# Batch 0 of an attention backward: rows of q and grad_out moved to SP's queue, and V's pieces transposed in another order

## The chip, the core and the metric

The kernel runs on one core of one Trainium2 chip. A core has TensorE (PE, with its weight loads shown apart as PEld), VectorE (DVE), ScalarE (ACT), GpSimd (POOL) and SyncE (SP), each with its own stream of instructions, and 16 DMA engines that all of them share. The metric is the device time of one execution in microseconds. Where a profile is shown, it is of one execution, and it gives the clock that TensorE was granted, as a share of its full speed.

## The reference

Attention with grouped heads, forward and backward, in bfloat16: 32 batches, 32 query heads, 4 key and value heads, 4 query positions, 2048 keys, head size 128. Eight query heads share a key head, so a batch has 128 query rows, 32 for each key head.

```python
def _fwd_reference(q, k, v):
    ...
    k = jnp.repeat(k, rep, axis=1)
    v = jnp.repeat(v, rep, axis=1)
    scale = D ** -0.5
    scores = jnp.einsum("bhqd,bhkd->bhqk", q, k) * scale
    p = _softmax(scores, axis=-1)
    return jnp.einsum("bhqk,bhkd->bhqd", p, v)

def reference(q, k, v, grad_out):
    ...
    _out, _vjp = jax.vjp(_f, q, k, v)
    _grads = _vjp(grad_out)
```

The outputs are the attention's output and the gradients of q, k and v. K and V are 2 MB a batch each, and so are their gradients; q, grad_out, the output and dq are 32 KB a batch each.

## The kernel before

The kernel goes through the batches one after the other, with the stages of neighbouring batches interleaved. A batch has these steps, and the names are those of the order that is written out in the kernel:

- `LK`, `LV`: load K and V, one transfer of 512 KB for each of the four key heads, on SP's queue. K has three buffers, V two.
- `KT0` to `KT7`, `VT0` to `VT7`: transpose K and V, in eight pieces each. A piece is eight 128x128 transposes on PE into one bank of PSUM, and one copy of 128x1024 to SBUF, by DVE, or by ACT where the name ends in `a`. Pieces with an even number are of heads 0 and 1, odd ones of heads 2 and 3.
- `QDT`: transpose q and grad_out. `Sa`, `Sb`: the two halves of the scores, and their row maxima on DVE (`m`); the second one also makes the bias of the exponentials (`negb`).
- `EXa`, `EXb`: the exponentials on ACT, with their row sums. `ETa`, `ETb`: their transposes on PE, and copies on DVE.
- `NRM`: the sum and the inverse of the row sums on DVE (`rinv`), then on POOL grad_out times `rinv` (`dop`, four instructions of 32 rows) and q times the scaled inverse (`qp`).
- `dV0` to `dV7`: the gradient of V from E and `dop`. `O`: the output, from E's transposes and V, and `delta`. `dPa`, `dPb`: grad_out times the transposed V, and the gradient of the scores (`ds`). `dSTa`, `dSTb`, `dQ`, `dK0` to `dK7`: the rest.

Every engine carries out its instructions in the order in which the text lists the steps; there is no scheduler behind it. `HEAD` (lines 17 to 25) lists the steps up to the third batch, `STEADY` one iteration of the middle, `TAIL` the end. A step is `name@batch`. PSUM has eight banks; a step takes one or two and gives them back once they are copied out, so a transpose may wait for a copy.

What matters for the first batch:

- q and grad_out come in groups of four batches (`GROUP`, line 192). The first group is loaded from ACT's queue in four transfers: 32 KB of q and of grad_out for batch 0, then 96 KB each for batches 1 to 3, in runs of 256 bytes. Later groups come by POOL's queue.
- Transfers from SP and ACT take turns in eight semaphores. A transfer whose semaphore is still held by an earlier one is issued only when that one has landed. In the kernel before, the four transfers of V of batch 0 wait in this way for q of batch 0, the first head of K, grad_out of batch 0, and the rows of q for batches 1 to 3; the second head of K of batch 1 waits for the rows of grad_out for batches 1 to 3.
- Ahead of the first data, PE runs 23 matmuls on the identity (line 212).

Of the kernel before, what the change touches and what calls it, by code (L numbers as in the profile page):

```python
# [14 lines left out]


HEAD = """
LK@0 LV@0 KT4@0 KT6@0 KT2@0 KT0@0 QDT@0 KT3@0 KT1@0 KT5a@0 KT7@0 LK@1 LV@1 Sa@0 Sb@0 VT2a@0 VT5@0 VT3@0 EXb@0 VT4@0 EXa@0 VT0a@0 ETb@0 ETa@0
NRM@0 VT7a@0 VT6@0 VT1a@0 QDT@1 KT4@1 KT6@1 KT2a@1 KT0@1 KT3@1 dV7@0 O@0 dV5@0 dPb@0 dV1@0 KT5@1 KT1@1 dV3@0 dV6@0 dPa@0 KT7@1 dV2@0 LK@2 LV@2
VT2@1 dV4@0 Sa@1 dV0@0 Sb@1 dK7@0 VT5@1 VT3@1 EXb@1 dSTa@0 VT4@1 EXa@1 VT0@1 QDT@2 dSTb@0 KT4@2 dK1@0 dK6@0 KT6@2 KT2@2 KT0@2 NRM@1 dK0@0 dQ@0  # L20
dK3@0 dK5@0 dK2@0 ETb@1 ETa@1 VT7@1 KT3@2 VT6@1 VT1@1 dV7@1 dK4@0 O@1 dV5@1 dPb@1 dV1@1 KT5@2 KT1@2 dV3@1 dV6@1 dPa@1 KT7@2 dV2@1 LK@3 LV@3
VT2@2 dV4@1 Sa@2 dV0@1 Sb@2 dK7@1 VT5@2 VT3@2 EXb@2 dSTa@1 VT4@2 EXa@2 VT0@2 QDT@3 dSTb@1 KT4@3 dK1@1 dK6@1 KT6@3 KT2@3 KT0@3 NRM@2 dK0@1 dQ@1
# [84 lines left out]
def kernel(ctx: ExitStack, tc: tile.TileContext, q, k, v, grad_out, out_0, out_1, out_2, out_3):  # L107
    nc = tc.nc
# [8 lines left out]
    W = 4  # L117
# [32 lines left out]
    q_f = q.rearrange("b h s d -> b (h s) d")  # L150
    go_f = grad_out.rearrange("b h s d -> b (h s) d")
# [10 lines left out]
    def late():  # L162

        return "v" in st.get(B - 1, {})
# [6 lines left out]
    def counted(n, i, *transfers):  # L171
        if late():
            return
        ends[n, i] = True
        for t in transfers:
            t.then_inc(sems[n][i % 4], 16)
            tc.no_tile_sem_insts.add(t.ins.name)
            tc.add_to_no_dep_group(f"{n}.{i}", t.ins)
            counts[n][i % 4] += 16
# [10 lines left out]
    groups = {}  # L190

    def GROUP(g, queue):

        groups[g] = []
        for name in ("q_sb", "do_sb"):
            groups[g].append(qd_pool.tile([P, W, D], BF16, name=name))
        for a, b in ((0, 1), (1, W)) if g == 0 else ((0, W),):
            for x, src in zip(groups[g], (q_f, go_f)):
                t = queue.dma_start(out=x[:, a:b], in_=src[g * W + a:g * W + b].rearrange("w p d -> p w d"))
                if g:  # L200
                    counted("qdo", g, t)

    def LK(b):
        S = st[b] = {}
        if b == 0:
            GROUP(0, nc.scalar)

            first = sm_pool.tile([P, 1], FP32, name="first")
            nc.scalar.activation(out=first[:], in_=ident[:, 0:1], func=ACT.Exp)
            t = banks.take(1)  # L210
            for _ in range(WARM_MATMULS):
                nc.tensor.matmul(
                    banks.ap(t)[:, 0, 0:2 * D], lhsT=ident[:], rhs=pairs["dop", 0][:].rearrange("p a d -> p (a d)"), start=True, stop=True,
                )
            banks.give(t)
        S["q"], S["do"] = (x[:, b % W, :] for x in groups[b // W])
        if b and b % W == 0:
            fence("qdo", b // W)
        if b % W == W - 1 and b + 1 < B:
            GROUP(b // W + 1, nc.gpsimd)  # L220
        S["k"] = k_pool.tile([P, NH, C, D], BF16, name="k_sb")
        for h in range(NH):
            nc.sync.dma_start(out=S["k"][:, h].rearrange("p c d -> p (c d)"), in_=k_v[b, h])

    def LV(b):
        S = st[b]
        S["v"] = v_pool.tile([P, NH, C, D], BF16, name="v_sb")
        for h in range(NH):
            nc.sync.dma_start(out=S["v"][:, h].rearrange("p c d -> p (c d)"), in_=v_v[b, h])

    def bank16():

        t = banks.take(1)
        return t, banks.ap(t).rearrange("p a w -> p (a w)").bitcast(BF16).rearrange("p (u r) -> p u r", r=P)
# [189 lines left out]
    def dP(b, i):  # L424
# [6 lines left out]
        banks.give(t)  # L431

    table = {"LK": LK, "LV": LV, "QDT": QDT, "O": O, "dQ": dQ, "NRM": NRM}
    for i, c in enumerate("ab"):
        for n, f in (("S", S_), ("EX", EX), ("dP", dP), ("ET", ET), ("dST", dST)):
# [10 lines left out]
    for w in STEADY.split():  # L446
        ahead = 0
        for mark, n in (("+3", 3), ("+2", 2), ("+", 1), ("-2", -2), ("-", -1)):
            if w.endswith(mark):
                w, ahead = w[:-len(mark)], n  # L450
# [3 lines left out]
    with tc.manual_schedule():  # L454

        for w in HEAD.split():
            w, b = w.split("@")
# [5 lines left out]
        for w in TAIL.split():  # L463
            w, b = w.split("@")
# [33 lines left out]
```

## Time and profile before

| | |
|---|---|
| three runs, us | 682.58, 682.12, 685.99 |
| median, us | 682.58 |
| the profiled execution, us | 685.76 |
| its span from the first to the last instruction, us | 684.0 |
| mean granted TensorE clock in it | 0.994 |

The times in the profile count from the start of the span. A group of instructions is named by its line, its engine, its operation, what it writes and what it reads, with the shape and the count. A row of the chain has a start, a length and what the chain was in then. A wait is put down to the event that came last. "DMA share" is the time that packets took, as a share of 16 engines; it can pass 1 a little. For a transfer the time to landing counts from its issue.

### The profile page before, as it was taken

The numbers are of one execution on the slowest core, as the hardware profiler recorded it, in microseconds if no ns is written. First come the engines' busy times: TensorE is split into PE (matmuls) and PEld (weight loads), VectorE is DVE, ScalarE is ACT, GpSimd is POOL, SyncE is SP. The second block draws the span as 40 slices with busy tenths as digits, with TensorE's granted clock in tenths as the row PEclk, the third lists the DMA queues.
The fourth block names the chain that finished last, engine by engine and source line by source line (L and its number), as shares of the span: only waits on it lengthen the run. The fifth ranks groups of instructions, "written<-read, shape, count | busy, mean of one in ns | idle before, by whom it ended". The sixth has DMA issues, their size and how long they took to land.

```text
span 684.0 us, 28075 instructions
## 1 busy us (share of the span) xinstructions
PE 626.7 (92%) x12375; PEld 454.9 (67%) x12375; DVE 590.0 (86%) x997; ACT 569.5 (83%) x673; POOL 273.0 (40%) x457
## 2 busy tenths in 40 slices
PE   7999998999989999999999999999998999989984
PEld 5777765677666677666677666677666677666652
DVE  4899998889888888998889898889898889888895
ACT  3799897888878888988888888888888888986885
POOL 1354343543426343264443426354244542434310
PEclk9999999999999999999999999999999999999999
DMA  9999999999999999999999999999999999999888
GB/s 344 404 321 405 418 415 411 414 389 413 415 414 409 392 415 414 414 416 410 417 416 415 416 415 416 414 417 413 414 415 414 412 411 415 416 417 395 340 335 298
DMA packets 76971, 274.45 MB, mean 401 GB/s; under 512 B 8976, under 2 KB 9134, under 8 KB 76849
## 3 DMA queue, kind: packets, MB, share of 16 engines
q1 hardware_dynamic: 41120, 144.85, 53.0%
q0 software_dynamic: 34640, 127.55, 46.4%
q8 instruction: 96, 1.57, 0.8%
q10 hardware_dynamic: 1088, 0.26, 0.2%
q14 instruction: 27, 0.21, 0.1%
HBM read 136.31 MB, written 136.31 MB: 399 GB/s over the span
## 4 chain that ended last, share of the span: by engine, by line
PE 79%; DVE 6%; issue 5%; ACT 5%; DMA 3%; POOL 0%; ACTq 0%; SPq 0%; DVEq 0%; POOLq 0%
PE banks L250 32%; PE banks L386 19%; PE banks L267 9%; PE banks L333 9%; PE banks L317 8%; ACT dv L390 3%; DMA v_sb<-in_v_dram 2%; DVE ds L428 2%; ACT dk L390 2%; DVE vt L252 1%; DMA q_sb<-in_q_dram 1%; DVE kt L252 1%; PE banks L240 1%; DVE dk L390 1%; DVE m L280 1%
## 5 line engine op out<-in xcount | busy, mean ns | idle before, releaser
L390 ACT CAST dv<-banks 128x1024 bf16<-128x1024 f32 x254 | 244.3, 1027 | 60.3 <-PE banks L386 60.1
L390 ACT CAST dk<-banks 128x1024 bf16<-128x1024 f32 x251 | 246.4, 1023 | 19.1 <-PE banks L386 15.2
L252 DVE COPY kt<-banks 128x1024 bf16<-128x1024 bf16 x254 | 162.9, 679 | 14.3 <-PE banks L250 13.8
L252 DVE COPY vt<-banks 128x1024 bf16<-128x1024 bf16 x252 | 164.0, 680 | 4.6 <-PE banks L250 4.2
L250 PE MATMUL banks<-ident,v_sb 128*128 128x128 bf16 x2048 | 144.0, 220 | 16.0 <-ACT dv L390 10.1
L300 POOL TENSOR_SCALAR dop<-do_sb,rinv 32x128 bf16<-32x128 bf16 x124 | 74.1, 598 | 205.3 <-PE banks L386 152.2
L250 PE MATMUL banks<-ident,k_sb 128*128 128x128 bf16 x2048 | 143.1, 219 | 10.8 <-issue 7.3
L250 PEld LDWEIGHTS <-k_sb 128*128 128x128 bf16 x2048 | 119.4, 98 | 38.5 <-issue 37.7
L250 PEld LDWEIGHTS <-v_sb 128*128 128x128 bf16 x2048 | 122.2, 98 | 32.0 <-issue 26.0
L386 PE MATMUL banks<-dop,e 64*128 64x256 bf16 x1024 | 96.8, 274 | 8.0 <-issue 3.0
L428 DVE SCALAR_TENSOR_TENSOR ds<-banks,delta,e 128x1024 bf16<-128x1024 f32 x64 | 82.0, 1283 | 25.3 <-PE banks L267 25.3
L188 POOL DMA_DIRECT2D out_dram<-dv x56 | 39.2, 703 | 145.3 <-ACT dv L390 135.0
L386 PE MATMUL banks<-qp,ds 64*128 64x256 bf16 x1024 | 87.8, 272 | 2.9 <-DVE dk L390 1.2
L300 POOL TENSOR_SCALAR qp<-q_sb,srinv 32x128 bf16<-32x128 bf16 x128 | 77.7, 607 | 10.6
L291 ACT ACTIVATE e<-banks,negb 128x1024 bf16<-128x1024 f32 x64 | 70.7, 1111 | 11.2 <-DVE negb L283 11.1
L280 DVE TENSOR_REDUCE m<-banks 128x1 f32<-128x1024 f32 x64 | 75.2, 1213 | 1.6 <-PE banks L267 1.5
L386 PEld LDWEIGHTS <-e 64*128 64x128 bf16 x1024 | 34.0, 94 | 54.1 <-issue 37.3
L386 PEld LDWEIGHTS <-ds 64*128 64x128 bf16 x1024 | 42.1, 94 | 31.1 <-ACT dv L390 12.6
L319 DVE COPY et<-banks 128x1024 bf16<-128x1024 bf16 x64 | 41.8, 686 | 23.7 <-PE banks L317 23.3
L267 PE MATMUL banks<-vt,qdt 128*32 128x512 bf16 x512 | 41.3, 384 | 6.8 <-issue 4.3
L319 DVE COPY dst<-banks 128x1024 bf16<-128x1024 bf16 x64 | 43.4, 679 | 0.0
L267 PEld LDWEIGHTS <-qdt 128*32 128x32 bf16 x1024 | 18.9, 94 | 36.1 <-issue 34.7
(45 smaller groups left out, 505.3 us busy)
## 6 DMA issues: line engine op xcount, KB each, us to landing
k_sb<-in_k_dram SPq DMA_DIRECT2D x128, 512.0 KB, 10.9
v_sb<-in_v_dram SPq DMA_DIRECT2D x128, 512.0 KB, 16.0
out_dram<-dk POOLq DMA_DIRECT2D x29, 2048.0 KB, 19.8
out_dram<-dv POOLq DMA_DIRECT2D x17, 2048.0 KB, 20.7
out_dram<-dv POOLq DMA_DIRECT2D x13, 1024.0 KB, 18.1
out_dram<-dv POOLq DMA_DIRECT2D x13, 960.0 KB, 22.3
out_dram<-dk SPq DMA_DIRECT2D x2, 2048.0 KB, 7.6
out_dram<-dv SPq DMA_DIRECT2D x1, 2048.0 KB, 8.7
```

The costliest lines, as they stand in the source:

```text
L250: nc.tensor.transpose(out=ps[:, 4 * hh + j, :], in_=S[which][:, 2 * (i % 2) + hh, 4 * (i // 2) + j, :], identity=ident[:])
L252: copy(out=S[f"{which}t{i}"][:], in_=ps)
L267: nc.tensor.matmul(ps[G * h:G * h + G, a, :], lhsT=S["qdt"][:, col, G * h:G * h + G], rhs=xt[:, 4 * (h % 2):4 * (h % 2) + 4, :].rearrange( ...
L280: nc.vector.reduce_max(out=S["m"][:, i:i + 1], in_=S[f"s{i}"][1], axis=AX.X)
L291: nc.scalar.activation(out=S[f"e{i}"][:], in_=ps, func=ACT.Exp, bias=S["negb"][:], scale=scale, accum_out=S["l"][:, i:i + 1],)
L300: engine.tensor_scalar(out=t[r, h % 2, :], in0=src[r, :], scalar1=by[r, :], scalar2=None, op0=ALU.mult)
L317: nc.tensor.transpose(out=ps[:, u, :], in_=S[f"{src}{i}"][:, P * u:P * u + P], identity=ident[:])
L319: nc.vector.tensor_copy(out=S[f"{name}{i}"][:], in_=ps)
L333: nc.tensor.matmul(ps[G * h:G * h + G, :], lhsT=S[f"{xt}{c // 8}"][:, c % 8, G * h:G * h + G], rhs=S[kv][:, h, c, :], start=(c == 0), stop ...
L386: nc.tensor.matmul(ps[:, a, :, c, :], lhsT=S[f"{x}{i // 4}"][r, u:u + P], rhs=S[y][r, :, :], start=True, stop=True, tile_position=(2 * G * ...
L390: copy(out=S[name][:, :, 2 * i:2 * i + 2, :].rearrange("p h c d -> p h (c d)"), in_=banks.ap(t).rearrange("p a (j w) -> p (a j) w", j=2),)
L428: nc.vector.scalar_tensor_tensor(out=S[f"ds{i}"][:], in0=ps, scalar=S["delta"][:], in1=S[f"e{i}"][:], op0=ALU.subtract, op1=ALU.mult,)
```

## The change

Two things change, both for batch 0 only. The 96 KB each of q and grad_out for batches 1 to 3 are no longer issued from ACT's queue at the very start but from SP's, behind the four transfers of the first V and ahead of K of batch 1. The turns in the eight semaphores shift with that: of the first V's four transfers the first two now take fresh semaphores, and the other two wait for q of batch 0 and for the first head of K. And in `HEAD` the V pieces of heads 0 and 1 (4, 0 and 6, behind 2 as before) come first, with the exponentials between them; the pieces of heads 2 and 3 follow, 5 and 3 of them between the transposes of E, and piece 6 is no longer behind `NRM`.

```diff
 HEAD = """
-LK@0 LV@0 ... LK@1 LV@1 Sa@0 Sb@0 VT2a@0 VT5@0 VT3@0 EXb@0 VT4@0 EXa@0 VT0a@0 ETb@0 ETa@0
-NRM@0 VT7a@0 VT6@0 VT1a@0 QDT@1 KT4@1 ...
+LK@0 LV@0 ... LK@1 LV@1 Sa@0 Sb@0 VT2a@0 VT4@0 VT0a@0 EXb@0 VT6@0 EXa@0 VT5@0 ETb@0 VT3@0 ETa@0
+NRM@0 VT7a@0 VT1a@0 QDT@1 KT4@1 ...
...
     def GROUP(g, queue):
+
         groups[g] = []
         for name in ("q_sb", "do_sb"):
             groups[g].append(qd_pool.tile([P, W, D], BF16, name=name))
-        for a, b in ((0, 1), (1, W)) if g == 0 else ((0, W),):
-            for x, src in zip(groups[g], (q_f, go_f)):
-                t = queue.dma_start(out=x[:, a:b], in_=src[g * W + a:g * W + b].rearrange("w p d -> p w d"))
-                if g:
-                    counted("qdo", g, t)
+        rows(g, 0, W if g else 1, queue)
+
+    def rows(g, a, b, queue):
+        for x, src in zip(groups[g], (q_f, go_f)):
+            t = queue.dma_start(out=x[:, a:b], in_=src[g * W + a:g * W + b].rearrange("w p d -> p w d"))
+            if g:
+                counted("qdo", g, t)
...
     def LV(b):
...
             nc.sync.dma_start(out=S["v"][:, h].rearrange("p c d -> p (c d)"), in_=v_v[b, h])
+        if b == 0:
+            rows(0, 1, W, nc.sync)
```

More of the change, by code (lines that the diff above doesn't have):

```diff
@@ L17 @@
 HEAD = """
-LK@0 LV@0 KT4@0 KT6@0 KT2@0 KT0@0 QDT@0 KT3@0 KT1@0 KT5a@0 KT7@0 LK@1 LV@1 Sa@0 Sb@0 VT2a@0 VT5@0 VT3@0 EXb@0 VT4@0 EXa@0 VT0a@0 ETb@0 ETa@0
-NRM@0 VT7a@0 VT6@0 VT1a@0 QDT@1 KT4@1 KT6@1 KT2a@1 KT0@1 KT3@1 dV7@0 O@0 dV5@0 dPb@0 dV1@0 KT5@1 KT1@1 dV3@0 dV6@0 dPa@0 KT7@1 dV2@0 LK@2 LV@2
+LK@0 LV@0 KT4@0 KT6@0 KT2@0 KT0@0 QDT@0 KT3@0 KT1@0 KT5a@0 KT7@0 LK@1 LV@1 Sa@0 Sb@0 VT2a@0 VT4@0 VT0a@0 EXb@0 VT6@0 EXa@0 VT5@0 ETb@0 VT3@0 ETa@0
+NRM@0 VT7a@0 VT1a@0 QDT@1 KT4@1 KT6@1 KT2a@1 KT0@1 KT3@1 dV7@0 O@0 dV5@0 dPb@0 dV1@0 KT5@1 KT1@1 dV3@0 dV6@0 dPa@0 KT7@1 dV2@0 LK@2 LV@2
 VT2@1 dV4@0 Sa@1 dV0@0 Sb@1 dK7@0 VT5@1 VT3@1 EXb@1 dSTa@0 VT4@1 EXa@1 VT0@1 QDT@2 dSTb@0 KT4@2 dK1@0 dK6@0 KT6@2 KT2@2 KT0@2 NRM@1 dK0@0 dQ@0
```

## Prediction

> **What bounds the kernel now.** First the page: the span, the busy shares, the DMA slices and the chain that ended last.
>
> ```profile
> span 684.0 us, 28075 instructions
> PE 626.7 (92%) x12375; PEld 454.9 (67%) x12375; DVE 590.0 (86%) x997; ACT 569.5 (83%) x673; POOL 273.0 (40%) x457
> GB/s 344 404 321 405 418 415 411 414 389 413 415 414 409 392 415 414 414 416 410 417 416 415 416 415 416 414 417 413 414 415 414 412 411 415 416 417 395 340 335 298
> DMA packets 76971, 274.45 MB, mean 401 GB/s; under 512 B 8976, under 2 KB 9134, under 8 KB 76849
> PE 79%; DVE 6%; issue 5%; ACT 5%; DMA 3%; POOL 0%; ACTq 0%; SPq 0%; DVEq 0%; POOLq 0%
> ```
>
> PE is busy 92% and is 79% of the chain, but the DMA engines are full in all but the last slices. 274.45 MB over 32 batches is 8.58 MB a batch, 20.8 us at 413 GB/s. So in the middle PE and the DMA have about one length, and a gain at the head lasts only if both get ahead. The edit touches batch 0 alone, so next the chain over the first 60 us (start, length, what).
>
> ```profile
> 1.66 7.35 DMA q_sb<-in_q_dram
> 9.02 6.87 DMA v_sb<-in_v_dram
> 15.94 2.83 PE banks L250 x28
> 18.77 0.87 PE banks L317 x8
> 19.66 1.29 DVE et L319 x2
> 21.05 0.17 DVE rinv L308
> 21.48 0.61 POOL dop L300
> 24.19 0.38 PE banks L386 x3
> ```
>
> V's last head is issued at 9.02, when the rows of q for batches 1 to 3 land, and it lands itself at 15.9. Then come three V pieces, the two transposes of E, `rinv`, four `dop` products on POOL and the first dV matmul. **24.19 us**, where dV7 of batch 0 gets going, is the mark that I try to move: from there PE's order is the old one.
>
> **What the rows of q and grad_out cost.** DMA view of the first 60 us (packets, MB, share of 16 engines; issues with KB and us to landing), the same queue from 6 to 8.9 us, where it was densest, and three stretches (length, busy us of PE, PEld, DVE, ACT, POOL, granted clock, DMA share, GB/s):
>
> ```profile
> q10 hardware_dynamic: 1088, 0.26, 2.0%
> q_sb<-in_q_dram ACTq DMA_DIRECT2D x1, 32.0 KB, 3.8
> q_sb<-in_q_dram ACTq DMA_DIRECT2D x1, 96.0 KB, 7.3
> do_sb<-in_grad_out_dram ACTq DMA_DIRECT2D x1, 96.0 KB, 9.9
> q10 hardware_dynamic: 617, 0.15, 23.6%
> 2.00:9.00 7.00, 6.73 (x64) 5.36 (x62) 2.05 (x4) 1.49 (x2) 0.81 (x4) 1.00 1.00 366
> 12.00:16.00 4.00, 0.94 (x13) 0.59 (x12) 2.10 (x3) 2.84 (x4) 0.00 (x0) 1.00 1.03 407
> 16.00:20.00 4.00, 4.00 (x44) 4.00 (x45) 2.41 (x4) 1.48 (x3) 0.00 (x0) 0.57 1.03 409
> ```
>
> The late issue at 9.02 looks like the fault, but the DMA engines had not run dry: their share is 1.00 to 1.03 throughout. An earlier issue only queues longer. What the move can give is the time that the small packets took ahead of V: 2.0% of 60 us on each engine is 1.2 us for all of ACT's queue, three quarters of it these rows, **0.9 us**. (The densest stretch says the same: 23.6% of 2.9 us for 617 packets is 0.85 for 768. The dip to 366 GB/s against 407 over 7 us gives 0.7.) V's last head then lands at about 15.0. It can't land more than 1.2 us sooner, and not later than now unless SP's queue handles 256-byte packets worse than ACT's.
>
> Behind V these rows stand in SP's queue ahead of K of batch 1. The bytes ahead of that K are the same as now, so it should land as now. No trace shows such rows alone in a queue: the low end is their busy time, 0.9 us, no change for K; the high end is the 9.9 us that 96 KB of them took from issue to landing, K 9 us late. That time is near all other queues' packets, taken turn by turn (at 366 GB/s, the 0.15 MB in 2.9 us is a seventh of what moved), so I take a value by the low end, and allow K 1 us. SP issues two more instructions, ACT two less, 0.4 to 0.5 us each. SP's issues wait for earlier transfers (each takes a turn in eight semaphores): V's last two heads now wait for the first q rows (3.8 us after issue) and K's first head, both landed before 5, so all V is issued by about 5.4. ACT's two issues go, and nothing waits for them: its first copy is at 10.2.
>
> The Trainium skill, *DMA: Bandwidth & Descriptors*, section "Issuing engines are not separate DMA queues", says that DMAs of all issuing engines interleave on the same 16 engines and that spreading them saves only issue time. That speaks against any gain from a changed queue by itself; the trace agrees in that the engines were full, and it leaves the rows' own place in the line. By it alone V would land as now, which is the second rival.
>
> **What the order costs and gives.** V's pieces 4, 0 and 6 need heads 0 and 1 only; 3 and 5 need heads 2 and 3. Before, PE transposed piece 2 and stopped (busy 0.94 us from 12 to 16, above), with pieces 5, 3 and 4 ahead of E. No instruction is added or removed on PE, DVE, ACT or POOL. Timelines of ACT, DVE, POOL and PE (start, length, instruction, count, idle before):
>
> ```profile
> 9.55 1.87 DVE L252 COPY kt<-banks 128x1024 bf16<-128x1024 bf16 x3
> 11.53 2.36 DVE L280 TENSOR_REDUCE m<-banks 128x1 f32<-128x1024 f32 x2
> 13.92 0.21 DVE L283 TENSOR_SCALAR negb<-m 128x1 f32<-128x1 f32 x1
> 16.37 2.27 DVE L252 COPY vt<-banks 128x1024 bf16<-128x1024 bf16 x3 [2.24 <-PE banks L250]
> 12.51 1.01 ACT L252 COPY vt<-banks 128x1024 bf16<-128x1024 bf16 x1 [1.31 <-PE banks L250]
> 14.17 1.11 ACT L291 ACTIVATE e<-banks,negb 128x1024 bf16<-128x1024 f32 x1 [0.64 <-DVE negb L283]
> 21.48 2.65 POOL L300 TENSOR_SCALAR dop<-do_sb,rinv 32x128 bf16<-32x128 bf16 x4 [18.67 <-DVE rinv L308]
> 20.03 1.50 PE L250 MATMUL banks<-ident,v_sb 128*128 128x128 bf16 x24
> 21.48 2.40 PE L250 MATMUL banks<-ident,k_sb 128*128 128x128 bf16 x40
> ```
>
> DVE works without a gap up to `negb`, so `negb` stays at 14.13. From there, engine by engine:
>
> - PE: pieces 4, 0 and 6 follow piece 2, 24 transposes at 0.062 us (1.50/24), 1.5 us, done by about 13.9, beside the reduce on DVE.
> - ACT: piece 2 to 13.5, then piece 0 to 14.5. That is 0.35 us more than `negb` allows, so the two exponentials run 14.5 to 15.6 and 15.6 to 16.75.
> - DVE: pieces 4 and 6 at 0.68 each to 15.5, inside its old 2.24 us of idle; piece 5 (head 3 at 15.0 plus 0.5 of PE) to 16.2; E's second half to 16.9; piece 3 to 17.55; E's first half once PE has it (16.75 plus 0.9 at half clock) to 18.35; `ls` and `rinv` to 18.7. Before it was 21.2: **2.5 us earlier**.
> - POOL: `dop` 18.95 to 21.6, so dV7 could start at 21.65.
> - PE behind E: pieces 7 and 1 (16), QDT (2), K of batch 1 (40). At the half clock of 16 to 20 us a transpose takes 0.10 (2.83/28). I assume that stretch stays slow: it reaches 19.75 with all but about 38 transposes done, and these take 2.1 us at 0.056 to 0.06: **21.9**.
>
> So dV7 starts at about 22.0 instead of 24.19, **2.2 us earlier**. The price of the added tie, piece 0 ahead of the exponentials on ACT, is the 0.35 in it. The next limit is K of batch 1:
>
> ```profile
> k_sb<-in_k_dram SPq DMA_DIRECT2D x1, 512.0 KB, 8.1
> ```
>
> This is its last head, issued at 12.9 (window 12.95 to 13.3), landing at 21.0; piece 3 of K is transposed last of five and needs it. 21.0 plus 0.5 is 21.5, still under 21.9; if the rows in SP's queue make it 1 us late, it is 22.5, and 1.7 us of gain are left. If PE keeps its full clock, POOL sets 21.65: 2.5 us.
>
> The Trainium skill, *TensorE: Matmul & The Clock Gate*, Part 1, has the clock fall to half after an idle window of about 3.4 us. The trace agrees (0.57 behind a stretch with 0.94 us of work); no run here shows at how much work it stays up. With some 1.5 us of work in that stretch the rule's wording would rather leave the clock up, which makes the sum 2.5.
>
> **Does it last?** From 24 us on the work is the same, on PE's order. Stretches again, and SP's own waits (total, times, longest):
>
> ```profile
> 34.00:35.00 1.00, 1.00 (x21) 1.00 (x19) 1.00 (x2) 0.94 (x1) 0.07 (x1) 1.00 0.57 229
> 40.00:45.00 5.00, 5.00 (x133) 4.28 (x128) 3.94 (x9) 4.30 (x6) 3.90 (x8) 1.00 0.77 226
> 55.50:75.50 20.00, 19.08 (x390) 13.96 (x388) 18.34 (x32) 17.79 (x22) 7.14 (x12) 1.00 1.03 413
> 495.00:515.80 20.80, 19.39 (x390) 14.16 (x388) 18.13 (x31) 17.81 (x22) 9.82 (x17) 1.00 1.03 415
> SPq L223 <- PE banks L386: 24.9, 2, 13.1
> ```
>
> The DMA has slack only where it waits for PE: K of batch 3 needs a K buffer, dV of batch 0 must be copied. Against 412 GB/s, 34 to 35 loses 0.44 us and 40 to 45 loses 2.26: 2.7 us. If PE comes 2.2 us sooner, the first store and the next K are issued 2.2 us sooner, and that much of the 2.7 is filled. Then both PE and the full DMA run 2.2 us ahead to the end. The profiled run was 685.76 us (span 684.0 and 1.76 around it), 3.2 above the median 682.58; it becomes 683.6, and the median **680.4**. For this kernel 1% (6.8 us) is about what a measurement can tell from no change, so this counts as no change.
>
> **Rivals.**
> 1. *Swallowed later* (682.6). The DMA holds the middle at 20.8 us a batch, against 20.0 where no backlog stands yet; if the early 2.2 us turns into queueing rather than filled slack, the end is where it was. For it: share 1.03 in every later stretch. Against: the 2.7 us of slack.
> 2. *The move does nothing, the order does* (681.0). V's last head lands at 15.9 after all: piece 5 is then done on DVE at 17.05, `rinv` at about 19.3, and PE, with more of the chain at half clock, reaches dV7 at about 22.6: 1.6 us. The reverse, only the move counting, is 0.9 us: 681.7.
> 3. *Slower: PE runs into the loads.* If PE is 2.2 us ahead and the DMA isn't, each later K or V is met 2.2 us closer to its landing. Batch 9's K, and what one stall did elsewhere:
>
> ```profile
> 163.58 2.59 SPq L223 DMA_DIRECT2D k_sb<-in_k_dram  x4
> k_sb<-in_k_dram SPq DMA_DIRECT2D x1, 512.0 KB, 13.1
> 180.33 0.61 PE L250 MATMUL banks<-ident,k_sb 128*128 128x128 bf16 x8
> 95.80:118.60 22.80, 20.43 (x390) 13.94 (x386) 18.61 (x32) 18.19 (x22) 7.23 (x12) 0.93 1.03 413
> ```
>
> Its second head lands at 177.0 (163.9 plus 13.1) for a use at 180.3: 3.3 us, and it decides from the point where that is gone. A stall then costs itself and a drop of the clock: the batch from 95.8 took 22.8 instead of 20.0 to 20.8, at a mean clock of 0.93. That is 2.4 us over the 20.4 between these; two such batches more make 685.2, four 690. Against it: the chain has 3% of DMA in all, 20 us, and 14.2 of them are the two rows of the head. The same would come at once if the rows of q and grad_out held SP's queue for 9.9 us: K of batch 1 at 30, dV7 at 30.5, 6.3 us later than now, 688.9.
>
> **How the numbers follow.** Forecast 0.52 (679.6 to 681.2). Rival 1, 0.18. Rival 2 in both halves, 0.10. Rival 3, 0.15 (0.02 of it the held queue). More than the sum, because one of the long batches goes with the shift, 0.05 (678). The ends of the unknown costs (1.4 to 2.5 us) lie inside 680.1 to 681.2. For 8 in 10 the range must reach into the rivals and the unsteadiness of single batches: 677.5 to 685.8. Over 1% either way: faster needs three long batches to go, 0.03; slower is the far end of rival 3, 0.04.
>
> **What would show it.** In the profile after: V's last head issued by 5.4 and landing near 15.0; PE with the V pieces between 11.9 and 14; `rinv` near 18.7 instead of 21.2, `dop` near 19.0, dV7 near 22.0; the clock in 16 to 20 still about 0.57; K of batch 1 landing at 21 to 22; DMA above 300 GB/s from 40 to 45; and the same 20.0 to 20.8 us per batch. I am wrong if dV7 is not before 23, or if it is and the end doesn't follow; then the windows of the batches show where it was given back.

## The result, and the profile after

Over 11 runs of each, the kernel took 684.43 us before (682.12 to 686.65) and **680.85 us** after (680.04 to 682.42): a ratio of 0.995, 95% interval 0.9934 to 0.9966, which is 3.4 us less, 2.3 to 4.5. The forecast was 680.4 us. A second set of 11 runs of the changed kernel, beside the first experiments, gave 681.4 us and 0.9968 (0.9955 to 0.9981). The profiled execution took 680.64 us with a span of 678.9. The profile before was of a slower execution than most (685.76 us), so the two spans lie 5.1 us apart, the medians 3.6. One execution further down, 694.85 us of the kernel with unused matmuls at the head, was in a slower state of the chip and is left out of its ratio.

The page of the kernel after: span, busy shares, data rates in 40 slices, and the chain by engine.

```profile
span 678.9 us, 28075 instructions
PE 623.5 (92%) x12375; PEld 452.8 (67%) x12375; DVE 589.8 (87%) x997; ACT 569.2 (84%) x673; POOL 273.0 (40%) x457
GB/s 343 408 392 413 416 411 412 417 411 417 413 417 414 413 416 412 416 415 413 418 415 416 414 414 415 416 416 414 412 416 408 404 414 413 415 403 401 340 340 300
PE 70%; DMA 12%; ACT 6%; DVE 5%; issue 4%; POOL 1%; SPq 0%; ACTq 0%; DVEq 0%; POOLq 0%
```

The instructions are the same in number, and the busy times nearly so. The third slice, 321 GB/s before, is at 392. Most of DMA's 12% of the chain are two stores of dK late in the run, 28.8 and 27.5 us, which will come up again. The chain over the first 34 us of the kernel after (start, length, what):

```profile
3.37 7.87 DMA v_sb<-in_v_dram
11.26 9.50 DMA k_sb<-in_k_dram
20.80 0.40 PE banks L255 x4
21.20 0.36 PE banks L391 x4
21.56 1.01 PE banks L338 x64
```

V's last head and the `rinv`, `dop` steps are off the chain. It now goes by the last head of K of batch 1, which lands at 20.76, four transposes of it, and dV7 at 21.2, where 24.19 stood before. The same stretch in the timeline of the kernel after (start, length, engine, instruction, count, idle before and what ended it):

```profile
11.66 2.18 PE L255 MATMUL banks<-ident,v_sb 128*128 128x128 bf16 x36
14.04 0.40 PE L255 MATMUL banks<-ident,v_sb 128*128 128x128 bf16 x4 [0.20 <-DMA v_sb<-in_v_dram]
13.54 0.21 DVE L288 TENSOR_SCALAR negb<-m 128x1 f32<-128x1 f32 x1
13.68 1.88 DVE L257 COPY vt<-banks 128x1024 bf16<-128x1024 bf16 x3
18.05 0.16 DVE L313 RECIPROCAL rinv<-ls 128x1 f32<-128x1 f32 x1
18.49 2.65 POOL L305 TENSOR_SCALAR dop<-do_sb,rinv 32x128 bf16<-32x128 bf16 x4 [15.67 <-DVE qdt L247]
20.80 0.40 PE L255 MATMUL banks<-ident,k_sb 128*128 128x128 bf16 x4 [0.60 <-DMA k_sb<-in_k_dram]
21.14 0.43 PE L391 MATMUL banks<-dop,e 64*128 64x256 bf16 x4
```

PE transposes four and a half pieces of V on end, waits 0.2 us for V's last head (2.40 before), and DVE copies without its old 2.24 us of idle. And the stretches that the prediction was made from, in the kernel after (length, busy us of PE, PEld, DVE, ACT, POOL, granted clock, DMA share, GB/s):

```profile
12.00:16.00 4.00, 2.84 (x48) 2.49 (x46) 3.52 (x6) 3.69 (x5) 0.00 (x0) 1.00 1.07 367
16.00:20.00 4.00, 3.97 (x71) 3.73 (x68) 3.65 (x8) 2.80 (x5) 1.33 (x3) 1.00 1.03 410
34.00:35.00 1.00, 1.00 (x19) 1.00 (x19) 1.00 (x3) 1.00 (x2) 0.00 (x0) 1.00 1.04 422
40.00:45.00 5.00, 4.89 (x123) 3.09 (x124) 4.48 (x9) 4.02 (x6) 4.52 (x9) 1.00 1.02 390
55.50:75.50 20.00, 19.35 (x398) 14.05 (x398) 18.52 (x32) 17.96 (x22) 7.14 (x12) 1.00 1.03 414
```

The clock stays at 1.00 from 16 to 20, where it was 0.57. The DMA runs at 422 and 390 GB/s where it ran at 229 and 226. In the 20 us from 55.5 both kernels look alike. The whole stretch in which the DMA falls short, first in the kernel before, then in the kernel after:

```profile
30.00:56.00 26.00, 24.96 (x478) 18.14 (x474) 24.34 (x41) 23.72 (x30) 10.40 (x16) 1.00 0.95 345
```

```profile
30.00:56.00 26.00, 25.39 (x504) 19.38 (x506) 24.26 (x43) 23.04 (x29) 10.41 (x16) 1.00 1.02 399
```

Against 412 GB/s the kernel before loses 4.2 us of transfer here, the kernel after 0.8.

### The profile page after: what moved, and what is told of

It is laid out like the page before. It is cut to its first block, busy times and chain, and to the rows that moved or that the text cites. A ratio compares the mean times of both kernels' runs of the same rounds, so it can differ in the third digit from the quotient of the medians.

```text
span 678.9 us, 28075 instructions
## 1 busy us (share of the span) xinstructions
PE 623.5 (92%) x12375; PEld 452.8 (67%) x12375; DVE 589.8 (87%) x997; ACT 569.2 (84%) x673; POOL 273.0 (40%) x457
## 4 chain that ended last, share of the span: by engine, by line
PE 70%; DMA 12%; ACT 6%; DVE 5%; issue 4%; POOL 1%; SPq 0%; ACTq 0%; DVEq 0%; POOLq 0%
PE banks L255 29%; PE banks L391 17%; PE banks L338 9%; DMA out_dram<-dk 8%; PE banks L322 8%; PE banks L272 7%; ACT dv L395 5%; DMA v_sb<-in_v_dram 2%; DVE ds L433 2%; DMA k_sb<-in_k_dram 1%; ACT dk L395 1%; DVE kt L257 1%; PE banks L245 1%; DVE dk L395 1%; DVE vt L257 1%
## 5 line engine op out<-in xcount | busy, mean ns | idle before, releaser
L257 DVE COPY kt<-banks 128x1024 bf16<-128x1024 bf16 x254 | 163.2, 680 | 12.1 <-PE banks L255 11.6
L255 PE MATMUL banks<-ident,v_sb 128*128 128x128 bf16 x2048 | 142.9, 219 | 12.7 <-ACT dv L395 10.2
```

The lines of the kernel that those rows point to most:

```text
L255: nc.tensor.transpose(out=ps[:, 4 * hh + j, :], in_=S[which][:, 2 * (i % 2) + hh, 4 * (i // 2) + j, :], identity=ident[:])
L257: copy(out=S[f"{which}t{i}"][:], in_=ps)
```

## The experiments

The theory: the end comes sooner by as much as the head does, because the DMA had slack at 34 to 45 us that only waited for PE; the rows' place and the order of V's pieces each free a wait of their own. The rivals: the order does it all; the change of queue does it all; the head's lead is swallowed in the middle. As a mark of the head I take the start of O of batch 0 in each profile, the step behind dV7. It was at 24.49 us before and at 21.49 after:

```profile
24.49 1.08 PE L333 MATMUL banks<-v_sb,et 128*32 128x128 bf16 x64
```

```profile
21.49 1.08 PE L338 MATMUL banks<-v_sb,et 128*32 128x128 bf16 x64
```

The mark is of one profile each, and it moves by up to 0.9 us with the same head: another profile with the old head has it at 23.83, four more with the changed head from 21.47 to 22.38. The GB/s from 30 to 56 us are the mark of the filled slack.

**The changed kernel again**, beside its parts.

> The changed kernel itself, on the same chip as the parts. All theories: 3.4 us under the kernel before, within 1.2; dV7 of batch 0 near 21.1 us, V's last head landing near 14.0, K of batch 1 complete near 20.8.

Measured: 2.2 us under the kernel before (ratio above), O at 21.90, V's last head landing at 14.26, K of batch 1 at 20.7. The two sets of runs put the gain at 2 to 3.5 us.

**The order alone**: the kernel before with the two changed lines of `HEAD`.

```diff
-... VT2a@0 VT5@0 VT3@0 EXb@0 VT4@0 EXa@0 VT0a@0 ETb@0 ETa@0
-NRM@0 VT7a@0 VT6@0 VT1a@0 ...
+... VT2a@0 VT4@0 VT0a@0 EXb@0 VT6@0 EXa@0 VT5@0 ETb@0 VT3@0 ETa@0
+NRM@0 VT7a@0 VT1a@0 ...
```

> The old place of the rows (ACT's queue, at the start), the new order of V's pieces. Theory 'both parts count, each frees a wait of its own': V's last head still lands near 15.9, rinv near 19.3, dV7 at 22.2 to 22.6 instead of 24.2; the end 1.6 to 2.0 us under the kernel before. Rival 'the order does it all': dV7 near 21.1 and the end 3.4 under. Rival 'the clock does it': the TensorE clock stays up in 16 to 20 us here too, since PE has work while it waits; if it drops to about 0.57, dV7 comes after 22.5.

Measured: ratio 0.998 (0.9959 to 1.0001), 1.4 us less. The chain of this kernel, then PE's timeline in it:

```profile
9.81 6.94 DMA v_sb<-in_v_dram
```

```profile
12.59 2.18 PE L250 MATMUL banks<-ident,v_sb 128*128 128x128 bf16 x36
16.80 0.40 PE L250 MATMUL banks<-ident,v_sb 128*128 128x128 bf16 x4 [2.02 <-DMA v_sb<-in_v_dram]
23.33 1.08 PE L333 MATMUL banks<-v_sb,et 128*32 128x128 bf16 x64
```

The rows in their old place, V's last head lands at 16.75 (9.81 plus 6.94), and PE still waits 2.0 us for it, now with more work done. The mark comes 1.2 us sooner than before, although V landed 0.9 us later in this profile than in that of the kernel before, with the same transfers ahead of it; so these 1.2 us are rather too few. The clock stayed at 1.00 although the rows hadn't moved.

**The rows alone**: the changed kernel with the old two lines of `HEAD`.

```diff
-... VT2a@0 VT4@0 VT0a@0 EXb@0 VT6@0 EXa@0 VT5@0 ETb@0 VT3@0 ETa@0
-NRM@0 VT7a@0 VT1a@0 ...
+... VT2a@0 VT5@0 VT3@0 EXb@0 VT4@0 EXa@0 VT0a@0 ETb@0 ETa@0
+NRM@0 VT7a@0 VT6@0 VT1a@0 ...
```

> The rows in SP's queue behind the first V, the old order of V's pieces. Theory 'both count': V's last head lands near 14.0 (1.9 us earlier), pieces 5, 3 and 4 follow at once, dV7 near 22.3; the end 1.9 us under the kernel before, within 1. Rival 'the order does it all, the queue is indifferent': dV7 near 24 and no change of the end.

Measured: ratio 0.998 (0.9957 to 1.0003), 1.4 us less, with runs from 680.1 to 687.4. The chain of this kernel, then PE's timeline in it:

```profile
5.20 9.72 DMA v_sb<-in_v_dram
```

```profile
14.96 1.74 PE L255 MATMUL banks<-ident,v_sb 128*128 128x128 bf16 x28 [2.13 <-DMA v_sb<-in_v_dram]
22.03 1.08 PE L338 MATMUL banks<-v_sb,et 128*32 128x128 bf16 x64
```

V's last head lands at 14.92, and the mark comes at 22.03: 2.5 of the 3.0 us, from the rows' place alone. So the order doesn't do it all at the head. The two overlap, but not in the wait, of which 2.0 and 2.1 us are left in either: V lands 1.0 us sooner here, and the other 1.5 us are the clock, which either part alone keeps at 1.00 (below). How much of it reached the end these runs don't tell: the interval goes from 2.9 us less to 0.2 more. The profiled one, the slowest of them, has PE stalls of 1.9 us at 231, 2.2 us at 275 and 2.2 us at 480, each followed by a clock drop, and no cause for them that the profile names well. Neither interval of the two parts clears 1.0, so how the gain at the end splits between them stays open.

**The rows from ACT's queue, but later**: the changed kernel with the rows of batches 1 to 3 issued from ACT's queue again, but behind ACT's first copy of K.

```diff
-        if b == 0:
-            rows(0, 1, W, nc.sync)
...
+    def ROWS(b):
+        rows(0, 1, W, nc.scalar)
...
-... KT1@0 KT5a@0 KT7@0 ...
+... KT1@0 KT5a@0 ROWS@0 KT7@0 ...
```

> The changed kernel with the rows for batches 1 to 3 issued from ACT's queue after ACT's first copy (near 11 us) instead of from SP's queue. Theory 'what counts is that the small packets are not ahead of V': V's last head lands at 13.6 to 14.6, dV7 at 21.1 to 21.6, the end as for the changed kernel, within 0.8 us. Rival 'SP's queue is what counts': as with the order alone, dV7 past 22 and 1 to 2 us of the gain gone.

Measured: **slower**, 1.0058 (1.0036 to 1.008), 4.0 us more. Both theories missed this one. PE's timeline in this kernel, then its DMA issues from 10 to 24 us (KB each, us to landing), then the packets of SP's queue (q1) and ACT's (q10) from 15 to 21 us (packets, MB, share of 16 engines):

```profile
15.57 0.40 PE L253 MATMUL banks<-ident,v_sb 128*128 128x128 bf16 x4 [1.48 <-DMA v_sb<-in_v_dram]
23.14 0.29 PE L243 MATMUL banks<-ident,do_sb 128*128 128x128 bf16 x1 [3.73 <-DMA do_sb<-in_grad_out_dram]
28.16 1.50 PE L336 MATMUL banks<-v_sb,et 128*32 128x128 bf16 x64
```

```profile
q_sb<-in_q_dram ACTq DMA_DIRECT2D x1, 96.0 KB, 8.8
do_sb<-in_grad_out_dram ACTq DMA_DIRECT2D x1, 96.0 KB, 11.6
```

```profile
q1 hardware_dynamic: 602, 2.20, 93.6%
q10 hardware_dynamic: 599, 0.15, 11.7%
```

V's last head lands at 15.53, 1.3 to 1.5 us later than in the two profiles of the changed kernel and outside the 13.6 to 14.6 expected. But PE loses most on the rows themselves: they take 8.8 and 11.6 us, and QDT of batch 1 stands on PE ahead of everything else and waits 3.7 us for them. In SP's queue they took 9.0 and 8.9 us from their issue, most of it in line behind V, and landed at 15.25 and 15.63, 1.3 and 1.6 us after V's last head (0.4 and 0.7 us after it in the second profile). So it counts where these packets stand: in SP's line they add little more than what their bytes need, on a queue of their own they get about one turn for each packet of K and V. What the queue alone does is not shown, because the edit also issues the rows later, at 10.31 and 11.50 us instead of 6.29 and 6.72. O came 3.7 us after that of the kernel before, the end 4.0 us.

**The head's lead taken away on PE.** The changed kernel with matmuls whose result is unused ahead of dV7 of batch 0.

```diff
+    def JUNK(b, n=28):
+        i = min((j for j in range(8) if banks.free_[j]), key=lambda j: banks.released[j])
+        for _ in range(n):
+            nc.tensor.matmul(
+                banks.ap((i, 1))[:, 0, 0:2 * D], lhsT=ident[:], rhs=pairs["dop", 2][:].rearrange("p a d -> p (a d)"), start=True, stop=True,
+            )
...
-... KT3@1 dV7@0 O@0 ...
+... KT3@1 JUNK@0 dV7@0 O@0 ...
```

> The changed kernel with 28 extra matmuls of 128x256 on PE (3.0 us, their result unused) just ahead of dV7 of batch 0. Theory 'the head's lead passes to the end because the DMA has slack there that waits for PE': dV7 near 24.1, DMA idle near 35 and 40 to 45 us again, the end 3 us over the changed kernel, about that of the kernel before (within 1.2). Rival 'the gain arises later, by a luckier middle': the end within 1 us of the changed kernel.

Measured: ratio 1.0 (0.9975 to 1.0025) to the kernel before: the whole gain is gone, as the theory had it. PE's timeline, then stretches of this kernel, columns as above:

```profile
24.96 1.08 PE L339 MATMUL banks<-v_sb,et 128*32 128x128 bf16 x64
```

```profile
34.00:35.00 1.00, 1.00 (x21) 1.00 (x19) 0.96 (x4) 0.67 (x2) 0.54 (x1) 1.00 0.25 102
40.00:45.00 5.00, 4.01 (x86) 3.42 (x76) 3.45 (x9) 3.46 (x5) 3.53 (x7) 1.00 0.74 236
```

The two holes of the DMA are back (102 and 236 GB/s; 229 and 226 before, 422 and 390 after).

**The same work in the middle.** The 28 matmuls ahead of O of batch 15 instead, then 56 of them, the 28 once more, and the 28 in the kernel before.

```diff
             for w, ahead in steady:
+                if it == 15 and w == "O":
+                    table["JUNK"](it)
```

> The changed kernel with the same 28 extra matmuls (3.0 us of PE) ahead of O of batch 15, near 330 us. Theory 'the middle is held by the DMA': the DMA share stays at 1.02 to 1.03, later batches catch up, the end 0 to 1.2 us over the changed kernel. Rival 'PE holds the middle': 3.0 us over it.

> The changed kernel with the 28 extra matmuls ahead of O of batch 15, once more and with more rounds. If what the first such run showed is real: 4 to 6 us under the kernel before. If it was chance: 2.3 to 3.5 under, as the changed kernel.

> The changed kernel with 56 extra matmuls (6.0 us of PE) ahead of O of batch 15. Theory 'the DMA holds the middle, PE runs ahead of it and waits for it later': the end 0 to 2 us over the run with 28, still not over the changed kernel by more than 1. Rival 'the reserve of PE is no more than those 3 us': 3 us over the run with 28.

> The kernel before with the 28 extra matmuls (3.0 us of PE) ahead of O of batch 15. Theory 'the middle has 2 us to gain for any kernel here when PE falls back once': 1 to 3 us under the kernel before. Rival 'the gain with the extra matmuls needs the early head, or was chance': within 1 us of the kernel before. If PE held the middle: 3 us over it.

Measured, as ratios to the kernel before: 0.9918 (0.9888 to 0.9949) and 0.9957 (0.994 to 0.9975) for the same kernel with 28, 0.994 (0.992 to 0.9961) with 56, and 0.9989 (0.997 to 1.0008) for the kernel before with 28. A group of the first of these:

```profile
L442 PE MATMUL banks<-dop,ident 128*128 128x256 bf16 x28 | 3.2, 273 | 0.0
```

These 3 us, or twice as many, cost nothing in the middle, where at the head they cost the whole gain. PE does not hold the middle. The first set even looked 2 us faster than the changed kernel; the repetition (2.9 us under the kernel before) says that much of this was chance.

**What holding the clock is worth.** The kernel before with 20 unused matmuls where PE waits for V.

```diff
-... Sb@0 VT2a@0 VT5@0 ...
+... Sb@0 VT2a@0 JUNK@0 VT5@0 ...
```

> The kernel before with 20 extra matmuls of 128x256 on PE (2.1 us, result unused) behind V's piece 2, where PE waits for V's third and fourth heads. Theory 'half of PE's slowness from 16 to 20 us is the clock, and it is the idle stretch that drops it': the clock stays at 1.00 from 16 to 20, the 28 transposes behind V's last head take 1.6 to 1.9 us instead of 2.83, dV7 at 23.0 to 23.4 instead of 24.2, the end 0.8 to 1.2 us under the kernel before. Rival 'the clock's drop lies beside DVE's copies and costs nothing': dV7 near 24.2, no change.

Measured: ratio 0.9979 (0.9951 to 1.0008), 1.4 us less, the interval just short of clear. Stretches of this kernel, columns as above, then PE's timeline in it:

```profile
12.00:16.00 4.00, 3.06 (x34) 2.63 (x32) 2.22 (x3) 2.72 (x4) 0.00 (x0) 1.00 1.01 377
16.00:20.00 4.00, 3.82 (x69) 3.83 (x70) 3.35 (x8) 2.32 (x4) 0.00 (x0) 1.00 0.98 355
```

```profile
16.18 1.74 PE L251 MATMUL banks<-ident,v_sb 128*128 128x128 bf16 x28 [1.11 <-DMA v_sb<-in_v_dram]
23.24 1.08 PE L334 MATMUL banks<-v_sb,et 128*32 128x128 bf16 x64
```

The 28 transposes behind V's last head take 1.74 us instead of 2.83, and O comes 1.25 us sooner, although V landed no sooner (16.1). From V's landing to O it is 7.1 us, as with the rows alone, against 8.6 in the kernel before and 8.25 in the other profile with its head (the 28 matmuls in the middle): the drop costs 1.1 to 1.5 us.

In all these profiles the clock changes only at steps of 3.41 us. Here are such steps, two each: the kernel before, then the same with the 28 matmuls in the middle, then the rows alone.

```profile
12.93:16.34 3.41, 0.80 (x11) 0.63 (x12) 1.17 (x2) 2.77 (x5) 0.00 (x0) 1.00 1.03 405
16.34:19.75 3.41, 3.41 (x36) 3.41 (x34) 2.16 (x4) 1.07 (x3) 0.00 (x0) 0.50 1.03 410
```

```profile
13.37:16.78 3.41, 1.55 (x25) 1.38 (x26) 1.67 (x4) 2.68 (x5) 0.00 (x0) 1.00 0.99 376
16.78:20.19 3.41, 3.41 (x36) 3.41 (x34) 2.53 (x5) 1.01 (x1) 0.00 (x0) 0.50 1.01 401
```

```profile
13.20:16.61 3.41, 1.65 (x30) 1.65 (x31) 2.24 (x5) 2.76 (x5) 0.00 (x0) 1.00 1.07 388
16.61:20.02 3.41, 3.41 (x65) 3.41 (x63) 3.37 (x9) 2.94 (x3) 0.91 (x2) 1.00 1.02 405
```

All twelve drops of the fourteen profiles, those of the last microseconds aside, follow a step with 0.2 to 1.8 us of PE work; every step with less than 1.5 us was followed by one, none with more than 1.8, and between these there are both. So with the rows alone the clock was kept by little.

**A further step at the head.** The changed kernel with `dop` of batch 0 on DVE, and dV7, O and dV5 ahead of K's piece 3; then the same with the 28 matmuls in the middle.

```diff
-        paired(S, "dop", S["do"], S["rinv"], b, nc.vector if b == B - 1 else nc.gpsimd)
+        paired(S, "dop", S["do"], S["rinv"], b, nc.vector if b in (0, B - 1) else nc.gpsimd)
...
-... KT4@1 KT6@1 KT2a@1 KT0@1 KT3@1 dV7@0 O@0 dV5@0 dPb@0 ...
+... KT4@1 KT6@1 dV7@0 KT2a@1 KT0@1 O@0 dV5@0 KT3@1 dPb@0 ...
```

> The changed kernel with dop of batch 0 made by DVE instead of POOL, and dV7, O and dV5 ahead of K piece 3 of batch 1. Theory 'the head's lead passes on only as far as the DMA has slack': dV7 near 20.2 and O near 20.5 to 21 (0.5 to 1.2 us sooner than the changed kernel), the end 0.3 to 1.0 under the changed kernel, so 3.0 to 4.4 under the kernel before. Rival 'DVE's extra work costs as much': no gain on the changed kernel.

> The kernel with dop of batch 0 on DVE, with the 28 extra matmuls (3.0 us of PE) ahead of O of batch 15. Theory 'that kernel loses its head because PE runs so far ahead that ACT waits for output buffers, PE with it, and the clock falls': with PE held back once the long waits of ACT for stores (4.8 and 2.6 us) do not come, the end is 3 to 5 us under the kernel before. Rival 'its changed head costs the time by itself': as without the extra matmuls, within 1.5 us of the kernel before.

Measured: 1.0004 (0.9977 to 1.003) without the matmuls, with runs from 680.4 to 688.9; **0.9937** (0.9913 to 0.9961) with them, 680.25 us. dV7 came at 19.4, 1.8 us sooner than in the changed kernel, but O only at 21.17 and 21.36, because two more pieces of K (16 transposes, 1.1 us) stand ahead of it in this order. ACT's timeline of the first of the two, and its stretch from 500 to 600 us, then that stretch of the one with the matmuls and of the changed kernel's second set:

```profile
502.18 1.01 ACT L395 CAST dk<-banks 128x1024 bf16<-128x1024 f32 x1 [2.55 <-DMA out_dram<-dk]
579.79 1.01 ACT L395 CAST dv<-banks 128x1024 bf16<-128x1024 f32 x1 [4.82 <-DMA out_dram<-dv]
```

```profile
500.00:600.00 100.00, 90.28 (x1750) 66.80 (x1747) 81.75 (x142) 80.17 (x96) 39.23 (x64) 0.95 1.02 400
```

```profile
500.00:600.00 100.00, 89.55 (x1852) 66.46 (x1850) 85.27 (x149) 83.29 (x100) 42.61 (x71) 1.00 1.02 412
```

```profile
500.00:600.00 100.00, 90.38 (x1861) 67.36 (x1859) 85.18 (x149) 83.78 (x100) 44.18 (x72) 1.00 1.03 412
```

Up to 500 us this profile is level with the changed kernel's. Then ACT finds no free output buffer, waits 2.6 and 4.8 us for old stores to land, PE stops with it, the clock is at half for 10.2 us in all, and the DMA moves 400 GB/s over the 100 us instead of 412, at no lower share. With the matmuls ahead of it, waits for stores are still there, 11.1 us in all (10.3 without), the longest 2.7 us, but no clock drop before the last microseconds. So my expectation that they would not come was wrong. That the long ones cost the time, by way of the clock, rests on this pair of profiles, and one speaks against it: the repetition with 28 matmuls in the middle has a wait of 3.7 us, no clock drop, and an end 2.9 us under the kernel before. The table of all:

| kernel | O of batch 0 starts, us | DMA from 30 to 56 us, GB/s | end against before, us |
|---|---|---|---|
| before | 24.5 | 345 | 0 |
| after, two sets | 21.5, 21.9 | 399, 395 | -3.4, -2.2 |
| order alone | 23.3 | 372 | -1.4 |
| rows alone | 22.0 | 392 | -1.4 |
| rows from ACT, late | 28.2 | 308 | +4.0 |
| after, 3 us of PE at the head | 25.0 | 326 | 0.0 |
| before, clock held | 23.2 | 373 | -1.4 |
| after, 3 us of PE in the middle, two sets | 21.5, 21.5 | 398, 399 | -5.6, -2.9 |
| after, 6 us in the middle | 22.4 | 381 | -4.1 |
| before, 3 us in the middle | 23.8 | 365 | -0.8 |
| `dop` on DVE | 21.2 | 397 | +0.3 |
| `dop` on DVE, 3 us in the middle | 21.4 | 389 | -4.3 |

The ends are the ratios above, less 1, times the 684 us of the kernel before; their intervals are 0.9 to 2.1 us to either side. Each 10 GB/s from 30 to 56 us are 0.6 us of transfer (26 us times 10, by 412). Apart from `dop` on DVE without the matmuls, the kernels whose DMA falls less short there than before end sooner, and the two whose DMA falls further short don't.

## Why the prediction was right

**The forecast and its way.** 2.2 us less was forecast and 3.4 and 2.2 were measured; the way by the head and the filled slack of the DMA holds. That 680.4 lies so near the measured 680.85 is luck in part: the median of three executions from which it starts, 682.58, is 1.9 us under that of eleven, and the gain was put 1.2 us under that of the first set. The step "from there PE's order is the old one, and both get ahead" was tested by the 3 us on PE at the head and by the late rows: +3.5 and +6.7 us at the mark against the changed kernel became +2.2 to 3.4 and +6.2 to 7.4 at the end. The 2.7 us that I counted as slack at 34 to 45 us were nearly all filled. The count was too small: the kernel before also fell short from 45 to 52 us (346 GB/s), and over 30 to 56 us 3.4 and 3.2 us were filled in the two profiles of the changed kernel, so more than 2.7 could pass on. That a measurement tells 1% at best was too cautious: eleven executions of each gave 0.5% with 0.16% to either side.

**The head, term by term.** The sum gave dV7 at 22.0; it came at 21.2. In the second profile three of its four matmuls waited for POOL until 21.6, which is the 21.65 of the prediction for a full clock. Three terms were mis-sized, all of them too late.
- *The clock.* I assumed that the stretch from 16 to 20 us stays slow. It ran at 1.00, with 2.84 us of PE work in the stretch before (0.94 in the kernel before). That is the rule of the Trainium skill, *TensorE: Matmul & The Clock Gate*, Part 1, by which an idle window drops the clock and the wording of which I had weighed and not followed; by it the sum was 2.5 us. The trace agrees in the main, but the step ahead of the drop held 0.80 us of work and was not idle throughout. My 1.5 us for the work ahead of that stretch were pieces 4, 0 and 6 alone; the rest of piece 2 and half of piece 5 were done in it too. The filled wait shows the price of the drop in the kernel before: 1.1 to 1.5 us, more than the 0.3 that my sum kept for it.
- *V's last head.* 15.0 was forecast, from 0.9 us of small packets, and 1.2 us sooner as the most that could be; it landed at 14.0 and 14.3, which is 1.9 and 1.6 us sooner, and at 14.9 with the rows alone. The third head came 0.6 us sooner (12.5 against 13.1; 0.2 in the second profile), within the estimate; the rest is the fourth, 1.5 us behind the third instead of 2.8. In the kernel before one of its sixteen parts came 1.5 us after the other fifteen, in the two profiles of the changed kernel 0.2 and 0.1 us, with the rows alone 1.1 us again. The change doesn't aim at that, so the larger part of this gain was luck. In each of these four profiles a 16 KB load of instructions was on the DMA for 1.1 to 1.2 us between 12.7 and 14.9; that this load was the cause is not tested. The late part then stays: of the last head of K of batch 1, which O now waits for, fifteen parts are there at 19.71 and the sixteenth at 20.76.
- *`rinv`.* 18.7 forecast for its end, 18.2 measured. `negb` in this one profile starts 0.4 us sooner than in the kernel before (13.54 against 13.92); in the second profile of the changed kernel it starts at 14.11, and `rinv` runs from 18.4 to 18.6.

**The rows in SP's queue.** K of batch 1 landed at 20.8, 21 to 22 forecast: the rows cost their own busy time, and the value by the low end was right. The two landed 1.3 and 1.6 us after V's last head (0.4 and 0.7 in the second profile). The Trainium skill's section that all issuing engines share the 16 DMA engines, cited in the prediction, did not decide it. Another section of that page of the Trainium skill, *DMA: Bandwidth & Descriptors*, "Queues, rings and completion order", says that each DMA engine goes round the queues packet by packet. The trace of the late rows agrees: 599 packets of ACT's queue against 602 of SP's from 15 to 21 us. On a queue of their own, beside K and V, 96 KB of 256-byte rows took 7.3 to 11.6 us from issue to landing; in line behind V both together added under 2 us after V. I had this as the 9.9 us of the high end, but as a danger of the new place; it was the cost of the old one, and the late rows from ACT's queue showed what it does when PE waits for them.

**The rivals.** "The order does it, the move nothing" is out for the head: the rows alone brought 2.5 us of it. My split there was wrong, 1.6 for the order and 0.9 for the rows, against 1.2 and 2.5; in sum 3.7, of which 3.0 to be had together. The step that it lacked is the clock: the rows alone brought V 1.0 us sooner, near my 0.9, and the other 1.5 us came of the clock that stayed up. "Swallowed later" is out for the changed kernel, but it is what happened to the step with `dop` on DVE, and perhaps to the rows alone. "Slower, PE runs into the loads" named the wrong wall: what an early PE met was the stores, by way of ACT's output buffers. ACT waited for stores 5.4 and 4.4 us in the two profiles of the changed kernel, not at all in the kernel before.

**The middle** took 19.7 to 21.0 us for most batches, but less evenly than forecast: the lead of PE over the kernel before, by the first use of each K, was 2.8 to 3.4 us up to batch 5, 5.9 at batch 6, since the long batch of the kernel before (from 95.8) took 20.3 us here, up to 9 us near 440 us (K of batch 22 first used at 439.2 instead of 448.1), and 4.7 us at the last batch. Between 481 and 587 us three batches of the changed kernel took 21.4 to 22.6 us; the two long stores of dK (28.8 us from 471.7, 27.5 us from 514.4) overlap the first two of them. So a lead in the middle is not yet a gain, and the 5.1 us between the two profiles hold a long batch that not every execution has.

## What to carry to other kernels

When PE and the DMA are both near full, look for the stretches where the DMA idles for want of an instruction, since here only what filled these shortened the run: 3 us of PE at the head were worth the whole gain, and the same 3 us in the middle nothing. Try small-row transfers in the line of the queue that carries the large ones, behind what is needed first and ahead of what is needed later; on a queue of their own they took 7.3 to 11.6 us here, and a step that needed them waited. Judge a gain at the head by several profiles, because a pipeline that is full can give it back far away.

## What was not expected

- The wait of the first batch cost twice: 2.4 us of idle, and then the clock. PE with 0.94 us of work from 12 to 16 us was at 0.57 in the next 4 us, and with 1.47 at 0.60 (the kernel before with the matmuls in the middle), but with 1.87 (rows alone) and with 2.77 (order alone) at 1.00. The work was nearly all transposes, so these kept the clock up.
- The rows of 256 bytes, issued at 10.3 and 11.5 us from ACT, took 8.8 and 11.6 us to land at only 0.2 MB of 5.6 MB moved.
- A kernel whose head is no later can be slower and less steady: 680.4 to 688.9 us over the runs with `dop` on DVE, 678.2 to 681.0 once 3 us of useless work held PE back. The lowest medians, 679.0 and 679.1 us with 28 and with 56 unused matmuls, have intervals that overlap with that of the first set of the changed kernel. Whether holding PE back helps by itself, and why, stays open.
